# An adaLN transformer block: value rows permuted over partitions, one load of six rows a partition for each tile, value products out of place, and a new instruction order

## The chip, the cores and the metric

The kernel runs on one core of one Trainium2 chip. The core has TensorE (PE in the profile: matmuls; PEld is its weight load), VectorE (DVE), ScalarE (ACT), GpSimd (POOL), and SyncE (SP), which here only issues DMAs. The engines run side by side and meet at semaphores; each runs its own instructions in order. The metric is the time of one execution in microseconds on the device, median of several runs.

## The reference

One block of a diffusion transformer: 2048 tokens, width 512, 32 heads of 16, a sliding dilated attention in which each token sees itself and seven earlier tokens at distances 2, 4, ..., 14, and a gated FFN of width 1792. Inputs are bf16.

```python
mod = (silu(c) @ w_mod)            # six vectors of 512: sa, ca, ga, sb, cb, gb
h = layernorm(x) * (1 + ca) + sa
q, k, v = split(h @ wqkv)          # 32 heads of 16
# for each token and head: 8 logits q.k at distances 0, 2, ..., 14, softmax, sum of the 8 weighted v
x = x + ga * (attention(q, k, v) @ wo)
h = layernorm(x) * (1 + cb) + sb
x = x + gb * ((silu(h @ w1) * (h @ w3)) @ w2)
```

Tokens before the start are masked with -1e9.

## The kernel before

The 2048 tokens are 16 tiles (T) of 128, one token a partition. `_build` describes every operation once, with its engine, what it reads and writes and from which pool of buffers its result comes; a list written out at the end of the file (`ORDER`, and `SLOTS` for the buffers) fixes the order in which each engine issues its operations and the buffer each value takes. `place` and `synchronize` turn the list into instructions with semaphore waits. So the order is fixed by hand, or rather by an offline planner, and nothing is rearranged at run time.

The stages, which the order interleaves:

- Loads by SP: x (tiles 0 and 1 singly, 2 and 3 together, then four by four), `w_mod` in parts (the first 1024 columns in four quarters), `wqkv` in three parts, then `wo`, `w1`, `w3`, `w2`.
- Modulation (L482, L485 on PE): it needs the first four quarters of `w_mod`. [...]
- First layernorm: DVE makes statistics (L540, L541), POOL the reciprocal root (L545, L547), DVE normalises (L552), PE transposes (L612), and ACT or DVE applies scale and shift (L620, L627). The last group of four tiles is transposed by DMA instead.
- Projections: Q and K with the weights stationary, so that they come out with features on partitions and tokens along the row (L664, evicted by ACT at L672 and L673), V with tokens on partitions (L683, evicted at L693). Each V tile is stored to a scratch tensor in DRAM, one DMA of 128 rows a tile.
- Attention, in blocks of two tiles (the last of four). *Logits*: DVE multiplies q by k, eight offsets at once (L714, 4096 elements a partition); PE sums the 16 features of a head with a 0/1 matrix into four groups of 32 partitions (L725, 16 matmuls of 32 rows a tile). *Softmax*: on DVE and ACT in PSUM (L737, L742, L755, L767, L769, L770), then a 32 by 32 transpose on DVE (L774), which leaves the weights in the order of V's rows. *Values*: four DMAs of 256 KB a tile load V from the scratch tensor with each pair of tokens' eight offsets spread over partitions (1 MB a tile, each V row eight times), DVE multiplies in place by the weights (L796), PE sums the eight offsets with a 0/1 matrix (L805), ACT evicts (L811), a DMA transposes, PE multiplies by `wo` (L829), and DVE adds to x and sums the row for the second layernorm (L833).
- Second layernorm: DVE and POOL make bias and scale (L562 nm, L572, L573, L574 nb), ACT squares and normalises (L566, L577), the first two groups of two tiles are transposed by PE, the others by DMA (four DMAs a group) and scaled by ACT (L597).
- FFN in groups of tiles 0 to 1, 2 to 3, 4 to 7, 8 to 11 and 12 to 15: up and gate (L845), activation (L851), product (L855, L856, L859), down (L888, and L876 in half rows for tiles 14 and 15), residual on DVE (L904), and one store a tile, or a half tile for 14 and 15.

V-load buffers: two of 8 KB a partition, and a third one laid over `wqkv` once that is no longer needed (`vsh_x`). Logits products have two buffers, V tiles six, attention weights three, output rows four.

The code around the V load and its product is this:

```python
        for q in range(4):
            p.dma(lambda q=q: vv.at[:, 2 * q:2 * q + 2, :],
                  bass.AP(v_dram, (PAD + T * P + 32 * q) * D, [[2 * D, 16], [-DIL * D, W], [1, 2 * D]]), ...
        def av(e):
            a_w = bass.AP(val.at, i * 8 * H, [[2 * 8 * H, P], [H, 8], [0, DH], [1, H]])
            v_w = bass.AP(vv.at, 0, [[8 * D, P], [D, 8], [H, DH], [1, H]])
            return e.tensor_tensor(v_w, v_w, a_w, ALU.mult)
```

Of the kernel before, what the change touches and what calls it, by code (L numbers as in the profile page):

```python
# [7 lines left out]
ALU = mybir.AluOpType  # L8
# [62 lines left out]
def packet_ns(size):  # L71
    return {256: 18, 512: 27, 768: 36, 1024: 48, 2048: 92}[size]


class Program:
# [41 lines left out]
    def dma(self, out, in_, key, packets, r=(), w=(), part=(), after=(), eng="sp", cost=450, group=None, transpose=False,  # L117
# [13 lines left out]
        ns = 600 if transpose else each * ((PACKET if pre == () and not SHIFTED else 84) if again else packet_ns(size)) + 170 * len(pre)  # L131
# [139 lines left out]
PACKET = 122  # L271
SHIFTED = False
# [3 lines left out]
AVCOL = frozenset(range(16))  # L276
# [5 lines left out]
def _build(p, A_x, A_wqkv, A_wo, B_w1, B_w3, B_w2, c, w_mod, out):  # L282
# [4 lines left out]
    x_view = x2d.rearrange("(t p) d -> p t d", p=P)  # L287
# [14 lines left out]
    vb = [sb([P, D], bf, f"v{i}") for i in range(6)]  # L302
    vshb = [sb([P, 8, D], bf, f"vsh{i}") for i in range(2)]
    pqb = [sb([P, W, KT, P], bf, f"pq{i}") for i in range(2)]
    NSM = 3
    atb = [sb([P, 2, 32, W], bf, f"attn{i}") for i in range(NSM)]
    alb = [sb([P, 2, 8, H], bf, f"al{i}") for i in range(3)]
# [9 lines left out]
    ind = sb([P, 2, 16, 2], bf, "ind")  # L317
    before = sb([P, 2, W, 4, 8], bf, "before")
# [27 lines left out]
    vsh_x = nc.alloc_sbuf_tensor_at("sb_vshx", [P, 8, D], bf, offset=nc.lookup_mloc(wqkv).addr)  # L346

    v_dram = nc.dram_tensor("v_scratch_dram", (PAD + S, D), bf)
    skew = nc.dram_tensor("skew_dram", (NT, 16, 4160), bf) if SHIFTED else None
# [48 lines left out]
    p.op("pool", lambda e: e.memset(ind[:], 0.0), 100, k, w=[vind])  # L398
    for r in range(2):
        p.op("pool", lambda e, r=r: e.memset(ind[:, r, :, r], 1.0), 100, k, w=[vind])  # L400
    for edge, mult in ((0, 1), (W - 1, -1)):
        p.op("pool", lambda e, edge=edge, mult=mult: e.affine_select(
            out=ind[:], in_=ind[:], compare_op=ALU.is_ge, fill=0.0, base=edge, pattern=[[0, 2], [-W * mult, 16], [0, 2]],
            channel_multiplier=mult), 250, k, w=[vind])
    p.op("pool", lambda e: e.memset(before[:], 0.0), 250, k, w=[vbefore])
    for q in range(2):
        p.op("pool", lambda e, q=q: e.affine_select(out=before[:, q], in_=before[:, q], compare_op=ALU.is_ge, fill=BEFORE, base=8 * q,
                                                    pattern=[[-DIL, W], [32, 4], [1, 8]], channel_multiplier=0), 400, k, w=[vbefore])
# [11 lines left out]
    def split_rows(a, row):  # L420
        return bass.AP(a.tensor, a.offset + row * D, [[D, 2], [2 * D, P // 2], [1, D]])

    for T in range(2):
        p.dma(x_sb[:, T, :], x_view[:, T, :], ("load", 1), (128, 1024), w=[vx[T]])
# [3 lines left out]
    p.dma(x_sb[:, 2:4, :], x_view[:, 2:4, :], ("load", 27), (256, 1024), w=vx[2:4])  # L428
# [4 lines left out]
    for g in range(1, 4):  # L433
        p.dma(x_sb[:, 4 * g:4 * g + 4, :], x_view[:, 4 * g:4 * g + 4, :], ("load", 5 + g), (512, 1024), w=vx[4 * g:4 * g + 4])
# [216 lines left out]
    def proj_qk(gi, Ts, kind, vh):  # L651
# [6 lines left out]
        for ft in range(KT):  # L658
            k = ("qk"[kind], 4 * gi + ft)
            vp = Val("ps_qk", psum)  # L660

            def mm(e, ts, ft=ft, vp=vp):
                for t in ts:
                    ins = e.matmul(bank(vp)[:, 0:n], wqkv[:, t, kind * D + ft * P:kind * D + (ft + 1) * P], vh.at[:, t, 0:n],  # L664
                                   start=(t == ORDER[0]), stop=(t == ORDER[-1]))
                return ins

            proj(mm, n, k, vh, vp, vwq[kind])

            def ev(e, ft=ft, vp=vp):  # L670
                if kind == 0:
                    return e.activation(dstv.at[:, ft, at0:at0 + n], bank(vp)[:, 0:n], ACT.Copy, scale=SCALE)  # L672
                return e.activation(kT[:, ft, PAD + 512 * cch + at0:PAD + 512 * cch + at0 + n], bank(vp)[:, 0:n], ACT.Copy)  # L673

            p.op("act", ev, c_act(n), k, r=[vp], part=[dstv])

    def proj_v(T, tt, vh):
        k = ("v", T)
        vp = Val("ps_v", psum)

        def mm(e, ts):
            for t in ts:
                ins = e.matmul(bank(vp), vh.at[:, t, tt * P:(tt + 1) * P], wqkv[:, t, 2 * D:3 * D], start=(t == ORDER[0]),  # L683
                               stop=(t == ORDER[-1]))
            return ins

        proj(mm, D, k, vh, vp, vwq[2])
        vt = Val("v", vpool)

        def ev(e):  # L690
            dst = bass.AP(vt.at, 0, [[D, P], [H, DH], [1, H]])
            src = bass.AP(PALL, bank(vp).offset, [[8 * 512, P], [1, DH], [DH, H]])
            return e.activation(dst, src, ACT.Copy)  # L693

        p.op("act", ev, c_act(512), k, r=[vp], w=[vt])
        vd = Val("vd")
        p.dma(v_dram[PAD + T * P:PAD + (T + 1) * P, :], lambda: vt.at[:], k, (128, 1024), r=[vt], w=[vd], cost=400, store=True)
        vv_dram[T] = vd
# [4 lines left out]
    def logits(Ts):  # L703

        vl = Val("ps_l", psum)
        for i, T in enumerate(Ts):
# [10 lines left out]
            def red(e, i=i, T=T, vp=vp):  # L717
                c0 = vl.at * 512 + i * W * 32
                if T == 0:
                    for q in range(2):  # L720
                        e.matmul(PALL[32 * q:32 * q + 32, c0:c0 + W * 32], ones[:, 0:32], before[:, q].rearrange("p w c t -> p (w c t)"),
                                 start=True, stop=False, tile_position=(0, 32 * q))
                for ft in range(KT):
                    for q in range(4):
                        ins = e.matmul(PALL[32 * q:32 * q + 32, c0:c0 + W * 32], E_sb[:, ft, :], bass.AP(vp.at, ft * P + 8 * q, [[W * KT * P, P], [KT * P, W], [32, 4], [1, 8]]),  # L725
                                       start=(ft == 0 and (T > 0 or q > 1)), stop=(ft == KT - 1), tile_position=(0, 32 * q))
# [35 lines left out]
    def softmax(Ts, vl, ve, vx_):  # L762
# [7 lines left out]
        p.op("dve", lambda e: e.tensor_tensor(ve.at[0][:, 0:n], bass.AP(PALL, bank(vl).offset, [[8 * 512, P], [W * 32, n], [1, 32], [32, W]]),  # L770
                                              bass.AP(ve.at[2], 0, [[64, P], [32, n], [1, 32], [0, W]]), ALU.mult),
             74 + 267 * n, k, r=[vr, vx_], w=[va], hold=[ve, vl], lead=o, lock=False)
        val = Val("al", alpool)
        p.op("dve", lambda e: e.transpose(bass.AP(val.at, 0, [[2 * 8 * H, P], [H, 2], [2 * H, 4 * n], [1, H]]),  # L774
                                          bass.AP(ve.at[0], 0, [[2 * W * 32, P], [8, 2], [16, 16 * n], [1, 8]])),
             60 + 267 * n, k, r=[va], w=[val], hold=[ve], lead=o, lock=False).again = True
        return val

    def values(T, i, val):

        vv = Val("vsh", vshpool)
        loads = []
        for q in range(4):
            pre = []
            if SHIFTED and q == 0:
                for a, b in ((0, 12), (12, 16)):
                    pre.append((bass.AP(skew, (T * 16 + a) * 4160, [[4160, b - a], [1, 4096]]),
                                bass.AP(B_w2.tensor, B_w2.offset + (T % 7 * 16 + a) * 8192, [[8192, b - a], [1, 4096]])))
            p.dma(lambda q=q: vv.at[:, 2 * q:2 * q + 2, :],
# [251 lines left out]
```

## Time and profile before

| | us |
|---|---|
| median of three runs | 244.26 |
| lowest, highest | 243.66, 245.57 |
| profiled execution, own time | 243.52 |
| profiled execution, span | 241.1 |
| granted clock, mean | 0.993 |

The span runs from the first to the last instruction of the profiled execution. "Busy" is the time in which an engine had an instruction under way; matmuls overlap, so the mean duration of one is longer than the distance from one to the next, and a busy PE can still be waiting for a fraction of a microsecond between two of them. A line such as `L796 DVE ... x12 | 27.3, 2286 | 4.2 <-DMA ...` is a group: line of the kernel, engine, output and input, count, busy time in us, mean ns of one, and the idle time of the engine just before these instructions with what ended it. SPq is SP's queue: the time to issue a DMA, not to move its data. Most of the DMA traffic is V loads (16 tiles of 1 MB); the attention spreads from about 24 to 182 us of the span, and PE runs projections and FFN around it.

### The profile page before, as it was taken

The numbers are of one execution on the slowest core, as the hardware profiler recorded it, in microseconds if no ns is written. First come the engines' busy times: TensorE is split into PE (matmuls) and PEld (weight loads), VectorE is DVE, ScalarE is ACT, GpSimd is POOL, SyncE is SP. The second block draws the span as 40 slices with busy tenths as digits, with TensorE's granted clock in tenths as the row PEclk, the third lists the DMA queues.
The fourth block names the chain that finished last, engine by engine and source line by source line (L and its number), as shares of the span: only waits on it lengthen the run. The fifth ranks groups of instructions, "written<-read, shape, count | busy, mean of one in ns | idle before, by whom it ended". The sixth has DMA issues, their size and how long they took to land.

```text
span 241.1 us, 4282 instructions
## 1 busy us (share of the span) xinstructions
PE 233.3 (97%) x1670; PEld 119.8 (50%) x1670; DVE 172.3 (71%) x281; ACT 153.2 (64%) x305; POOL 26.8 (11%) x55
## 2 busy tenths in 40 slices
PE   6699999999999999999899999999999999999995
PEld 1468644444576768564344344443334444444464
DVE  6599999999998999999999896518423414213832
ACT  2369665889998996772897759644576952242100
POOL 3354930001002000121000001100002000000000
PEclk9799999999999999999999999999999999999999
DMA  5999999499599699499996516872040021100011
GB/s 161 356 298 343 270 285 242 105 304 345 178 228 271 196 270 216 92 215 137 253 248 154 162 33 149 140 210 70 0 122 11 22 67 48 42 0 0 0 57 54
DMA packets 44123, 38.30 MB, mean 159 GB/s; under 512 B 19512, under 2 KB 34888, under 8 KB 44104
## 3 DMA queue, kind: packets, MB, share of 16 engines
q1 hardware_dynamic: 44096, 38.04, 61.9%
q8 instruction: 13, 0.21, 0.4%
q14 instruction: 6, 0.05, 0.1%
q10 hardware_dynamic: 8, 0.00, 0.0%
HBM read 29.62 MB, written 4.21 MB: 140 GB/s over the span
## 4 chain that ended last, share of the span: by engine, by line
PE 77%; DMA 8%; DVE 6%; ACT 4%; SPq 2%; POOL 1%; issue 1%; DVEq 0%
PE pall L845 34%; PE pall L888 13%; PE pall L664 11%; PE pall L683 6%; PE pall L829 4%; DMA sb_vsh<-v_scratch_dram 3%; PE pall L876 3%; PE pall L805 2%; PE pall L725 2%; DMA sb_wm_s<-in_w_mod_dram 2%; SPq L127 2%; PE pall L612 2%; DMA sb_h<-sb_xn 1%; ACT sb_xn L577 1%; DMA sb_ot<-sb_oa 1%; ACT sb_h L597 1%
## 5 line engine op out<-in xcount | busy, mean ns | idle before, releaser
L845 PE MATMUL pall<-sb_h,sb_w 128*128 128x512 bf16 (+1 forms) x560 | 102.3, 337 | 0.8 <-ACT sb_h L597 0.7
L845 PEld LDWEIGHTS pall<-sb_h,sb_w 128*128 128x128 bf16 x560 | 51.5, 98 | 49.6 <-ACT sb_sg L851 4.9
L851 ACT ACTIVATE sb_sg<-pall 128x512 bf16<-128x512 f32 (+1 forms) x70 | 34.7, 517 | 26.7 <-PE pall L845 19.7
L888 PE MATMUL pall<-sb_w,sb_hh 128*128 128x512 bf16 x196 | 44.7, 379 | 0.2 <-DVE sb_w L929 0.2
L714 DVE TENSOR_TENSOR sb_pq<-sb_q,sb_kT 128x4096 bf16<-128x4096 bf16 x16 | 36.3, 2282 | 0.2 <-ACT sb_q L672 0.2
L855 ACT ACTIVATE sb_hh<-pall 128x256 bf16<-128x256 f32 (+1 forms) x56 | 26.3, 495 | 7.8 <-PE pall L845 7.8
L664 PE MATMUL pall<-sb_h,sb_wqkv 128*128 128x512 bf16 (+1 forms) x160 | 31.1, 337 | 0.0
L888 PEld LDWEIGHTS pall<-sb_w,sb_hh 128*128 128x128 bf16 x196 | 18.9, 98 | 23.1 <-ACT sb_sg L851 0.9
L796 DVE TENSOR_TENSOR sb_vsh<-sb_vsh,sb_al 128x4096 bf16<-128x4096 bf16 x12 | 27.3, 2286 | 4.2 <-DMA sb_vsh<-v_scratch_dram 4.2
L904 DVE TENSOR_TENSOR sb_o<-pall,sb_x 128x512 bf16<-128x512 f32 (+1 forms) x18 | 11.1, 629 | 19.6 <-PE pall L888 13.2
L856 DVE TENSOR_TENSOR sb_hh<-sb_sg,sb_hh 128x256 bf16<-128x256 bf16 (+1 forms) x56 | 18.0, 349 | 6.4 <-ACT sb_hh L855 4.4
L859 DVE TENSOR_TENSOR sb_hh<-sb_sg,pall 128x512 bf16<-128x512 bf16 x14 | 8.9, 684 | 16.0 <-PE pall L845 16.0
L664 PEld LDWEIGHTS pall<-sb_h,sb_wqkv 128*128 128x128 bf16 x160 | 14.2, 98 | 11.9 <-ACT sb_kT L673 0.6
L620 ACT ACTIVATE sb_h<-pall,sb_modc 128x256 bf16<-128x256 bf16 (+1 forms) x22 | 13.7, 666 | 9.2 <-DVE sb_modc L495 7.2
L572 POOL TENSOR_SCALAR sb_rs<-sb_var 128x2 f32<-128x2 f32 x8 | 3.3, 423 | 145.6 <-ACT sb_xn L566 145.6
L597 ACT ACTIVATE sb_h<-sb_h,sb_modc 128x512 bf16<-128x512 bf16 x16 | 11.8, 804 | 10.1 <-DMA sb_h<-sb_xn 10.1
L833 DVE SCALAR_TENSOR_TENSOR sb_x<-pall,sb_x 128x512 bf16<-128x512 f32 x16 | 10.8, 681 | 8.7 <-PE pall L829 8.5
L829 PE MATMUL pall<-sb_wo,sb_ot 128*128 128x512 bf16 x64 | 16.5, 380 | 0.1
L683 PE MATMUL pall<-sb_wqkv,sb_h 128*128 128x512 bf16 x64 | 16.4, 387 | 0.0
L577 ACT ACTIVATE sb_xn<-sb_x,sb_nb,sb_rs 128x512 bf16<-128x512 bf16 x16 | 12.5, 822 | 3.0 <-DVE sb_nb L574 3.0
L566 ACT ACTIVATE sb_xn<-sb_x,sb_nm 128x512 bf16<-128x512 bf16 x16 | 11.4, 717 | 3.2 <-DVE sb_nm L562 3.2
L673 ACT ACTIVATE sb_kT<-pall 128x512 bf16<-128x512 f32 (+1 forms) x20 | 9.7, 521 | 3.3 <-PE pall L664 3.3
(82 smaller groups left out, 227.5 us busy)
## 6 DMA issues: line engine op xcount, KB each, us to landing
sb_vsh<-v_scratch_dram SPq DMA_DIRECT2D x48, 256.0 KB, 4.8
sb_vshx<-v_scratch_dram SPq DMA_DIRECT2D x16, 256.0 KB, 4.8
sb_w<-in_B_w_dram SPq DMA_DIRECT2D x6, 512.0 KB, 6.9
sb_w<-in_B_w_dram SPq DMA_DIRECT2D x6, 384.0 KB, 6.1
v_scratch_dram<-sb_v SPq DMA_DIRECT2D x16, 128.0 KB, 5.1
out_dram<-sb_o SPq DMA_DIRECT2D x14, 128.0 KB, 1.8
sb_wqkv<-in_A_wqkv_dram SPq DMA_DIRECT2D x3, 512.0 KB, 8.5
sb_x<-in_A_x_dram SPq DMA_DIRECT2D x3, 512.0 KB, 8.0
```

What stands on the lines that cost most here:

```text
L577: p.op("act", lambda e, vn=vn, T=T: e.activation(vn.at[:], x_sb[:, T, :], ACT.Identity, bias=nb[:, T, :], scale=rs[:, NT + T, :]), c_act(5 ...
L597: return e.activation(vh.at[:, ft, 0:n * P], vh.at[:, ft, 0:n * P], ACT.Identity, bias=modc[:, 8 * which + ft:8 * which + ft + 1], scale=m ...
L664: ins = e.matmul(bank(vp)[:, 0:n], wqkv[:, t, kind * D + ft * P:kind * D + (ft + 1) * P], vh.at[:, t, 0:n], start=(t == ORDER[0]), stop=(t ...
L683: ins = e.matmul(bank(vp), vh.at[:, t, tt * P:(tt + 1) * P], wqkv[:, t, 2 * D:3 * D], start=(t == ORDER[0]), stop=(t == ORDER[-1]))
L714: return e.tensor_tensor(vp.at[:], in0, in1, ALU.mult)
L796: return e.tensor_tensor(v_w, v_w, a_w, ALU.mult)
L829: ins = e.matmul(bank(vy), vt.at[:, ft, :], wo[:, ft, :], start=(ft == 0), stop=(ft == KT - 1))
L845: ins = e.matmul(bank(vp)[:, 0:n], wt[:, t, fi * P:(fi + 1) * P], vh.at[:, t, 0:n], start=(t == 0), stop=(t == KT - 1))
L851: p.op("act", lambda e: e.activation(vt.at[:, 0:n], bank(vgp)[:, 0:n], ACT.Silu), c_act(n), k, r=[vgp], w=[vt], table="silu")
L855: p.op("act", lambda e: e.activation(vh_.at[:, 0:n], bank(vup)[:, 0:n], ACT.Copy), c_act(n), k, r=[vup], w=[vh_])
L856: p.op("dve", lambda e: e.tensor_tensor(vh_.at[:, 0:n], vt.at[:, 0:n], vh_.at[:, 0:n], ALU.mult), 60 + n * 69 // 128, k, r=[vt], w=[vh_], ...
L888: ins = e.matmul(bank(vz), vhh[fi].at[:, tt * P:(tt + 1) * P], w2[:, fi, :], start=(fi == 0), stop=(fi == NF - 1))
```

## The change

Within a tile, token and partition are permuted: token 4j + c of a tile sits on partition 32c + j. To that end x is loaded in four DMAs of 32 partitions each (every fourth row), V is stored likewise, two tiles at a time with four DMAs a pair, Q and K are written back in token order by the eviction, and the output store puts the rows back in order with one DMA whose destination has four as its first dimension. Partition (j, pair of offsets) of the V load then needs six consecutive V rows: four tokens, at two offsets two rows apart. So one DMA a tile, with 6 KB a partition, replaces four with 2 KB, 768 KB instead of 1 MB a tile. DVE writes the value product to another buffer, taken from the pool of the logits products, which grows from two to three buffers; V-load buffers are freed by the product instead of by PE's reduction, and shrink to 6 KB. The softmax's last product is split in two, one for each half of the offsets, so that the DVE transpose reads and writes contiguously. The logits reduction reads its products with a step of four elements. The first-tile mask needs one matmul instead of two. V tiles have three buffers of two tiles (instead of six of one), attention weights two (instead of three). Some switches that had one setting are removed. `ORDER` and `SLOTS` are new throughout; among other things one third of `wqkv` is now the first DMA on SP, ahead of x, and value products and logits products are interleaved anew.

```diff
-    for T in range(2):
-        p.dma(x_sb[:, T, :], x_view[:, T, :], ("load", 1), (128, 1024), w=[vx[T]])
+    def load_x(T, n, key, engs):
+        loads = []
+        for c in range(4):
+            p.dma(x_sb[32 * c:32 * c + 32, T:T + n, :],
+                  bass.AP(x2d.tensor, x2d.offset + (T * P + c) * D, [[4 * D, 32], [P * D, n], [1, D]]), key, (32 * n, 1024),
+                  part=vx[T:T + n], eng=engs[c], group=loads)
+    load_x(0, 2, ("load", 1), ("sp", "sp", "sp", "sp"))
...
             def ev(e, ft=ft, vp=vp):
+                src = bass.AP(PALL, bank(vp).offset, [[8 * 512, P], [P, n // P], [32, 4], [1, 32]])
                 if kind == 0:
-                    return e.activation(dstv.at[:, ft, at0:at0 + n], bank(vp)[:, 0:n], ACT.Copy, scale=SCALE)
+                    return e.activation(bass.AP(dstv.at, ft * 512 + at0, [[KT * 512, P], [P, n // P], [1, 4], [4, 32]]), src,
+                                        ACT.Copy, scale=SCALE)
...
-        p.dma(v_dram[PAD + T * P:PAD + (T + 1) * P, :], lambda: vt.at[:], k, (128, 1024), r=[vt], w=[vd], cost=400, store=True)
+        for c in range(4):
+            p.dma(bass.AP(v_dram, (PAD + Ts[0] * P + c) * D, [[4 * D, 32], [P * D, 2], [1, D]]),
+                  lambda c=c: vt.at[32 * c:32 * c + 32, :, :], ("v", Ts[1]), (64, 1024), r=[vt], part=[vd], cost=400, store=True,
+                  group=stores)
...
-                        ins = e.matmul(PALL[32 * q:32 * q + 32, c0:c0 + W * 32], E_sb[:, ft, :], bass.AP(vp.at, ft * P + 8 * q, [[W * KT * P, P], [KT * P, W], [32, 4], [1, 8]]),
+                        ins = e.matmul(PALL[32 * q:32 * q + 32, c0:c0 + W * 32], E_sb[:, ft, :], bass.AP(vp.at, ft * P + 32 * q, [[W * KT * P, P], [KT * P, W], [1, 4], [4, 8]]),
...
+        for wf in range(2):
+            o = p.op("dve", lambda e, wf=wf: e.tensor_tensor(
+                bass.AP(ve.at[0], wf * 128, [[2 * W * 32, P], [W * 32, n], [1, 128]]),
+                bass.AP(PALL, bank(vl).offset + 32 * wf, [[8 * 512, P], [W * 32, n], [1, 32], [64, 4]]),
+                bass.AP(ve.at[2], 0, [[64, P], [32, n], [1, 32], [0, 4]]), ALU.mult),
...
-        for q in range(4):
-            p.dma(lambda q=q: vv.at[:, 2 * q:2 * q + 2, :],
-                  bass.AP(v_dram, (PAD + T * P + 32 * q) * D, [[2 * D, 16], [-DIL * D, W], [1, 2 * D]]), ("vl", T), (128, 2048),
+        p.dma(lambda: vv.at[:], bass.AP(v_dram, (PAD + T * P - 2) * D, [[4 * D, 32], [-4 * D, 4], [1, 6 * D]]), ("vl", T), (128, 6144),
+              r=[vv_dram[T]] + ([] if T % 2 else [vv_dram[T - 1]] if T else [vvpad]), w=[vv], cost=640, again=True)
+        vr = Val("pr", pqpool)
...
-            v_w = bass.AP(vv.at, 0, [[8 * D, P], [D, 8], [H, DH], [1, H]])
-            return e.tensor_tensor(v_w, v_w, a_w, ALU.mult)
+            v_w = bass.AP(vv.at, 2 * D, [[6 * D, P], [-2 * D, 2], [D, 4], [1, D]])
+            return e.tensor_tensor(bass.AP(vr.at, 0, [[8 * D, P], [1, 8 * D]]), v_w, a_w, ALU.mult)
...
-        finals.append(p.dma(out2d[T * P:(T + 1) * P, c0:c0 + n], lambda: vo.at[:, 0:n], ("zo", T), (128, 2 * n), r=[vo], cost=400, store=True))
+        finals.append(p.dma(bass.AP(out2d.tensor, out2d.offset + T * P * D + c0, [[D, 4], [4 * D, 32], [1, n]]), lambda: vo.at[:, 0:n],
+                            ("zo", T), (512, 2 * n), r=[vo], cost=400, store=True))
```

More of the change, by code (lines that the diff above doesn't have):

```diff
@@ L825, in values @@
+        p.dma(lambda: vt.at[:], lambda: va.at[:], ("ac", T), (128, 1024), r=[va], w=[vt], cost=1250, transpose=True)
         vy = Val("ps_y", psum)
@@ L916, in _build @@
         proj_qk(gi, Ts, 1, vh)
-        for i, T in enumerate(Ts):
-            proj_v(T, i, vh)
+        for i in range(0, len(Ts), 2):
+            proj_v(Ts[i:i + 2], (i, i + 1), vh)
     gate(0)
```

144 lines of the change are left out of this document (56 added, 88 removed), and 116 rows, old and new, of tables (ORDER, SLOTS).

## The prediction

> **What bounds the kernel now.** I read the page first (busy times, DMA slices), then the timeline of PE, then the waits of PE and DVE, the groups, and last the chain that ended last around 80 and 110 us.
>
> ```profile
> span 241.1 us, 4282 instructions
> PE 233.3 (97%) x1670; PEld 119.8 (50%) x1670; DVE 172.3 (71%) x281; ACT 153.2 (64%) x305; POOL 26.8 (11%) x55
> DMA  5999999499599699499996516872040021100011
> ```
>
> PE is busy for 233.3 of 241.1 us, so only 7.8 us of the span are PE idle. DMA is nearly full in most slices up to the 22nd (132 us) and light after. The PE timeline shows where the 7.8 us lie (start, length, line, count, idle before it):
>
> ```profile
> 1.81 2.32 PE L503 MATMUL pall<-sb_ones 128*128 128x512 bf16 x5 [1.81 <-DVE sb_ones L383]
> 8.47 0.18 PE L482 MATMUL pall<-sb_mbase,sb_ident 128*128 128x8 bf16 x1 [1.91 <-DMA sb_wm_s<-in_w_mod_dram]
> 10.17 1.27 PE L612 MATMUL pall<-sb_ident,sb_xn 128*128 128x128 bf16 x10
> 11.66 3.20 PE L683 MATMUL pall<-sb_wqkv,sb_h 128*128 128x512 bf16 x12
> ...
> 84.89 1.67 PE L888 MATMUL pall<-sb_w,sb_hh 128*128 128x512 bf16 x7 [0.20 <-DVE sb_w L929]
> ...
> 116.46 0.61 PE L805 MATMUL pall<-sb_vshx,sb_ind 128*32 128x512 bf16 x8 [0.22 <-DVE sb_vshx L796]
> 117.81 7.08 PE L845 MATMUL pall<-sb_h,sb_w 128*128 128x512 bf16 x32 [0.74 <-ACT sb_h L597]
> ...
> 152.69 7.72 PE L888 MATMUL pall<-sb_w,sb_hh 128*128 128x512 bf16 x35
> 160.25 1.03 PE L829 MATMUL pall<-sb_wo,sb_ot 128*128 128x512 bf16 x4
> ...
> 233.77 4.75 PE L876 MATMUL pall<-sb_w,sb_hh 128*128 128x256 bf16 x42
> ```
>
> Idle at the start is 1.81 + 1.91 plus 0.2; in the whole interior 0.20 + 0.22 + 0.74 = 1.2; at the end 241.1 - 238.5 = 2.6. A 512-column matmul in steady state takes (160.25 - 152.69)/35 = 0.216 us. Going through this timeline's rows from 16.71 us to the end (140 rows; first and last: 16.71 and 233.77) and comparing start-to-start times with count x 0.216 (half for 256 columns, a quarter for the 32-column reductions), 7.7 us are over: 3.8 at the 25 blocks of 32-column reductions, where PE changes its tiling (1.0 of it the two idles at 116 and 117), and 3.9 spread thinly. So the matmul work, which the change leaves alone, fixes about 230 us; a better order can win little more than the 1.2 us of idle and part of the 3.9.
>
> **The change, part by part.**
>
> *Start.* PE's first needed work is the modulation, released by the DMA of its weights.
>
> ```profile
> 0.79 1.39 SPq L127 DMA_DIRECT2D sb_x<-in_A_x_dram  x3
> 2.22 1.85 SPq L127 DMA_DIRECT2D sb_wm_s<-in_w_mod_dram  x4
> 6.00:12.00 6.00, 4.09 (x55) 2.89 (x54) 3.56 (x11) 1.83 (x5) 2.10 (x6) 0.76 1.03 356
> 12.12 0.69 DVE L540 BATCH_NORM_STATS2 sb_st<-sb_x 128x6 f32<-128x512 bf16 x1 [0.34 <-DMA sb_x<-in_A_x_dram]
> 24.50 2.29 DVE L714 TENSOR_TENSOR sb_pq<-sb_q,sb_kT 128x4096 bf16<-128x4096 bf16 x1 [0.22 <-ACT sb_q L672]
> ```
>
> (The third row is a window: busy time of PE, PEld, DVE, ACT, POOL, then clock 0.76, DMA share 1.03, 356 GB/s.) SP spends 1.85/4 = 0.46 us on an issue. Now the last quarter of the modulation weights is SP's 7th DMA, with 1.5 MB up to it; in the new order it is the 13th, with 2.0 MB (512 KB of wqkv went to the front, and each x load became four pieces). Issues end at 0.79 + 13 x 0.46 = 6.8 us, which is earlier than the bytes: 0.5 MB more at 356 GB/s is 1.5 us, so the last quarter comes at 8.5 + 1.5 = 10.0, its 8 matmuls and modc take some 0.4, and the first projection can start at about 10.8. Before, it started at 11.66, because PE did transposes for tiles 2 and 3 first (10.17); these eight (0.1 us each at that clock) now come later. Good end: -0.4. Bad end: if pieces of 32 partitions load at half the rate of whole tiles, 0.5 MB of x costs 1.5 us more: +1.1. No row shows the rate of a piece alone, so I take +0.2, nearer the good end, because the large wqkv transfer in front covers the small issues.
>
> *Middle.* x of tiles 4 to 7 has 3.0 MB up to its end instead of 2.5, so DVE's row at 12.12 moves by 1.5 us, of which the normalising of tiles 2 and 3 (moved into the gap) fills 0.8: DVE's first logits product (24.50) comes 0.7 to 1.5 us later. From there DVE is the engine that PE's order leans on:
>
> ```profile
> L714 DVE TENSOR_TENSOR sb_pq<-sb_q,sb_kT 128x4096 bf16<-128x4096 bf16 x16 | 36.3, 2282 | 0.2 <-ACT sb_q L672 0.2
> L796 DVE TENSOR_TENSOR sb_vsh<-sb_vsh,sb_al 128x4096 bf16<-128x4096 bf16 x12 | 27.3, 2286 | 4.2 <-DMA sb_vsh<-v_scratch_dram 4.2
> L770 DVE TENSOR_TENSOR sb_attn<-pall,sb_ssum 128x512 bf16<-128x512 f32 x8 | 5.5, 684 | 0.1
> L904 DVE TENSOR_TENSOR sb_o<-pall,sb_x 128x256 bf16<-128x256 f32 x4 | 1.7, 425 | 5.0 <-PE pall L876 5.0
> 82.78 7.77 DMA sb_vsh<-v_scratch_dram
> ...
> 109.23 0.17 DVE sb_nb L574
> ...
> 111.50 3.29 DMA sb_h<-sb_xn
> ...
> 114.82 2.94 ACT sb_h L597 x4
> ```
>
> The last four rows are from the chain: the normalising of tiles 6 and 7 (109.23), its transposes and ACT's scaling are what PE waits for at 117.81. Up to that nb instruction DVE runs 12 logits products, 9 value products and 5 softmaxes in both orders. The value product out of place costs what the logits product does (also out of place, also with a backward step: 2282 against 2286): nothing. The softmax's last product in two halves is 2 x 425 - 684 = +166 ns, 5 times by then, 0.8 us. What can go is DVE's wait for V, 4.2 us in all, 0.3 of it after that point: one 768 KB load replaces four of 256 KB, and the chain's V load took 7.77 us. Sum for the nb instruction: +0.7 to +1.5, +0.8, and between 0 and -3.9: from -2.4 to +2.3. The FFN of 117.81 moves with it, but not to before 116.5, where PE's own work ends: -1.3 to +2.3. I take 0, the middle.
>
> *SP's queue.* 64 V-load issues become 16, 16 V stores become 32, six x loads become 20.
>
> ```profile
> L127 SPq DMA_DIRECT2D sb_vsh<-v_scratch_dram x48: 515/594/1319, 20.3 to 159.7; - x48
> L127 SPq DMA_DIRECT2D v_scratch_dram<-sb_v x16: 344/588/1528, 16.0 to 124.5; - x16
> L693 ACT ACTIVATE sb_v<-pall 128x512 bf16<-128x512 f32 x16 | 9.4, 607 | 1.9 <-PE pall L683 1.9
> L672 ACT ACTIVATE sb_q<-pall 128x512 bf16<-128x512 f32 x12 | 6.8, 601 | 2.0 <-PE pall L664 2.0
> ```
>
> -48 x 0.594 + 16 x 0.588 + 14 x 0.46 = -12.7 us of SP time, spread; it acts only through the waits for V and the transposes, so it is in the range above. The first store of a pair now waits for the second tile's eviction (one more projection, 4 x 0.216, and 0.6 on ACT: 1.5 us); behind it stand V loads and transposes on SP, and DVE waits for those. SP's 12.7 us hide it; without them, up to 1.5 us at one place. Value products now take one of three buffers shared with the logits products; a product that finds none waits for PE's reduction, with DVE's whole queue behind it: at most one block of PE work (7 x 0.216 = 1.5 us), in the same range. Q and K are evicted with a rearranged write: V's eviction, rearranged on its read side, took 607 against 601 ns, so nothing; the fewer constants of POOL are hidden before 8.47.
>
> *End.* The output rows of a tile now go to four interleaved runs, the first dimension of the destination being four.
>
> ```profile
> out_dram<-sb_o SPq DMA_DIRECT2D x14, 128.0 KB, 1.8
> out_dram<-sb_o SPq DMA_DIRECT2D x4, 64.0 KB, 1.5
> sb_wo<-in_A_wo_dram SPq DMA_DIRECT2D x4, 128.0 KB, 7.2
> v_scratch_dram<-sb_v SPq DMA_DIRECT2D x16, 128.0 KB, 5.1
> ```
>
> 64 KB more cost 1.8 - 1.5 = 0.3 us. At best the last store stays at 1.5 us (0); if only a quarter of the DMA engines carries it, its moving part is 4 x 0.3 and the end comes 0.9 us later. No row shows such a store: +0.5, the middle. [...]
>
> *Sum:* +0.2 + 0 + 0.5 = +0.7. On the profiled execution (span 241.1, its own time 243.52) that is 244.2; that execution lies 0.74 under the median of the three times (244.26), so the median forecast is 245.0.
>
> **Rivals.**
>
> *The waits go and the order closes up (faster).* With the V waits gone, PE loses its 1.2 us of idle and some 2.4 of the 3.9 thin losses, and the start takes its good end: -3.6 - 0.4 + 0.5 = -3.5, 240.8. For it: DVE waits 4.2 us for V. Against it: PE was idle only 1.2 us while that happened.
>
> *x in 32-partition pieces loads at half the rate (slower).* All 2 MB of x at 178 instead of 356 GB/s take 5.9 us more. The start takes +1.1; tiles 4 to 15 reach DVE later, and after the cover that DVE's other work gives I put the first logits at 3.5 us later rather than 0.7 to 1.5; with 0.8 for softmax and half of the V waits gone (-2.0) the FFN at 117.81 moves by 2.3, and the last store by 0.9: +3.2, 247.5. It decides from about 250 GB/s downwards. For it: 32-partition loads of wo took 7.2 us for 128 KB, against 5.1 for the V stores; against it: both ran under a full DMA. [...]
>
> *The strided read slows the reductions (slower).* PE's logits reduction now reads its products with a step of four elements instead of runs of eight.
>
> ```profile
> 27.61 0.44 PE pall L725 x16
> ```
>
> Sixteen of them take 0.44 us, so the 256 take 7.0 us on PE; at half the rate that is +7.0, +7.7 with the forecast: 252. No row shows PE reading with such a step; it decides as soon as a reduction takes over 0.6 us.
>
> **How the numbers follow.** Forecast 0.50, closing up 0.20, half-rate x 0.22, strided read 0.08. The forecast's own range is the middle's -1.3 to +2.3 around 245.0: 243.7 to 247.3. Eight in ten: 240.8 leaves out the lower half of the first rival (0.10), 248.0 the strided read; 240.8 to 248.0. 1% (2.4 us) is about what a measurement can tell from no change: under 241.8 falls nearly all of the first rival, 0.19; over 246.7 fall most of the half-rate case, the strided read and a little of the forecast, 0.31; 0.50 remains.
>
> **What would show it.** Start: PE's first projection near 11.3 to 11.9, and the wait of DVE for x under 2.5 us. Middle: DVE's wait for V under 2 us, and the first 512-column FFN matmul within 2.3 us of 117.8. End: landing of a 64 KB store, 1.5 or over 2.2 us. Reductions: 16 in 0.44 us, or 0.9. The prediction is wrong if PE shows an idle of over 3 us in its interior, or if the thin losses fall below 2 us.

## The result, and the profile after

The changed kernel takes 265.38 us (median of four runs, 264.28 to 265.95) against 243.96 for the kernel before on the same chip: ratio 1.0865, 95% interval 1.0796 to 1.0935. The forecast was 245.0, its range 240.8 to 248.0. The change costs 21 us, more than any rival gave. Every ratio here divides the mean time by that of the kernel before run beside it (median 243.9 to 244.9 us from one session to the next) and leaves out the few executions in a slower state, which the ranges of times include.

The page of the changed kernel (the span, the engines' busy times, the chain that ended last):

```profile
span 263.5 us, 4267 instructions
PE 244.4 (93%) x1669; PEld 121.2 (46%) x1669; DVE 172.9 (66%) x289; ACT 169.8 (64%) x303; POOL 26.6 (10%) x52
q1 hardware_dynamic: 37448, 33.84, 45.2%
PE 69%; ACT 21%; DMA 5%; issue 1%; DVE 1%; SPq 1%; POOL 0%; POOLq 0%; DVEq 0%
```

The last two of these lines in the page of the kernel before (the queue that carries nearly all DMAs, and the chain):

```profile
q1 hardware_dynamic: 44096, 38.04, 61.9%
PE 77%; DMA 8%; DVE 6%; ACT 4%; SPq 2%; POOL 1%; issue 1%; DVEq 0%
```

PE now lacks 19.1 us of the span (7.8 before). ScalarE's busy time rose from 153.2 to 169.8 us, and it holds 21% of the chain (4% before). The DMA load fell as intended, by 4.2 of 38.0 MB, and that bought nothing that shows. (The V loads were 16.8 of these 38.0 MB, the largest part but less than half.) The groups of the lines that the change touched (kept apart by shape), and under them those of the kernel before that the prediction does not show:

```profile
L668 ACT ACTIVATE sb_q<-pall 128x512 bf16<-128x512 f32 x12 | 16.1, 1362 | 2.1 <-PE pall L659 2.1
L670 ACT ACTIVATE sb_kT<-pall 128x512 bf16<-128x512 f32 x12 | 15.4, 1374 | 1.4 <-PE pall L659 1.4
L670 ACT ACTIVATE sb_kT<-pall 128x256 bf16<-128x256 f32 x8 | 5.3, 796 | 2.0 <-PE pall L659 2.0
L668 ACT ACTIVATE sb_q<-pall 128x256 bf16<-128x256 f32 x8 | 5.2, 853 | 0.0
L726 PE MATMUL pall<-sb_pq,sb_E 128*32 128x256 bf16 x256 | 15.6, 393 | 0.0
L792 DVE TENSOR_TENSOR sb_pq<-sb_vsh,sb_al 128x4096 bf16<-128x4096 bf16 x13 | 29.5, 2285 | 1.5 <-PE pall L801 1.5
L772 DVE TENSOR_TENSOR sb_attn<-pall,sb_ssum 128x256 bf16<-128x256 f32 x16 | 6.5, 418 | 0.0
```

```profile
L672 ACT ACTIVATE sb_q<-pall 128x256 bf16<-128x256 f32 x8 | 3.1, 442 | 0.4 <-PE pall L664 0.4
...
L673 ACT ACTIVATE sb_kT<-pall 128x512 bf16<-128x512 f32 x12 | 7.0, 600 | 2.9 <-PE pall L664 2.9
L673 ACT ACTIVATE sb_kT<-pall 128x256 bf16<-128x256 f32 x8 | 2.7, 402 | 0.3 <-PE pall L664 0.3
...
L725 PE MATMUL pall<-sb_pq,sb_E 128*32 128x256 bf16 x256 | 8.9, 274 | 0.0
```

Two groups have become dear. A 512-column eviction of Q or K takes 1362 to 1374 ns instead of 600; the four eviction rows together hold ScalarE for 42.0 us, before 19.6 (with the 6.8 of Q's 512 columns). And a matmul of the logits reduction takes 393 ns on the mean instead of 274. The value product and the halves of the softmax product cost what the prediction said, and DVE's wait for V is gone.

PE's timeline (start, length, line, count, idle before it) shows where this lands:

```profile
11.94 2.32 PE L659 MATMUL pall<-sb_h,sb_wqkv 128*128 128x256 bf16 x10
...
28.01 1.04 PE L683 MATMUL pall<-sb_wqkv,sb_h 128*128 128x512 bf16 x4 [0.56 <-ACT sb_q L668]
...
61.51 1.04 PE L813 MATMUL pall<-sb_wo,sb_ot 128*128 128x512 bf16 x4 [0.59 <-ACT sb_kT L670]
...
64.48 1.92 PE L726 MATMUL pall<-sb_pq,sb_E 128*32 128x256 bf16 x32
...
77.14 1.04 PE L683 MATMUL pall<-sb_wqkv,sb_h 128*128 128x512 bf16 x4 [0.64 <-ACT sb_q L668]
...
137.65 7.08 PE L829 MATMUL pall<-sb_h,sb_w 128*128 128x512 bf16 x32
```

The first projection comes at 11.94 (before 11.66), the first 512-column FFN matmul at 137.65 (before 117.81). So 19.6 of the 22.4 us of span are lost between these two. Q, K and V are projected there until about 85 us, and PE's short waits name ScalarE's evictions: the idles that the whole timeline lists between 12 and 89 us add up to 9.2 us, 9.0 of them ended by an eviction of Q, K or V, where the kernel before had 1.2 us of idle in its whole interior. The same stretch in windows of 6 us (busy time of PE, PEld, DVE, ACT, POOL, each with its count; clock, DMA share, GB/s), first of the changed kernel, then of the kernel before:

```profile
24.00:30.00 6.00, 4.60 (x34) 2.62 (x32) 2.09 (x7) 6.00 (x11) 0.15 (x1) 1.00 0.93 324
54.00:60.00 6.00, 5.40 (x53) 2.42 (x51) 4.62 (x3) 6.00 (x9) 0.00 (x0) 1.00 0.62 109
```

```profile
54.00:60.00 6.00, 6.00 (x34) 2.94 (x33) 5.91 (x8) 6.00 (x13) 0.92 (x2) 1.00 1.05 344
```

The last row is one that the prediction should have shown: between 54 and 60 us ScalarE was already busy for all 6.00 us before the change (and for 5.98 and 5.94 us in the next two windows). Its 64% over the span is an average; in this stage it had no slack, so a surcharge on its evictions there can go straight into the time.

### The profile page after: what moved, and what is told of

It is laid out like the page before. It is cut to its first block, busy times and chain, and to the rows that moved or that the text cites. A ratio compares the mean times of both kernels' runs of the same rounds, so it can differ in the third digit from the quotient of the medians.

```text
span 263.5 us, 4267 instructions
## 1 busy us (share of the span) xinstructions
PE 244.4 (93%) x1669; PEld 121.2 (46%) x1669; DVE 172.9 (66%) x289; ACT 169.8 (64%) x303; POOL 26.6 (10%) x52
## 4 chain that ended last, share of the span: by engine, by line
PE 69%; ACT 21%; DMA 5%; issue 1%; DVE 1%; SPq 1%; POOL 0%; POOLq 0%; DVEq 0%
PE pall L829 35%; PE pall L872 11%; ACT sb_q L668 7%; ACT sb_kT L670 6%; PE pall L726 5%; PE pall L659 5%; PE pall L813 4%; PE pall L683 4%; PE pall L801 2%; DMA sb_ot<-sb_oa 2%; DMA sb_h<-sb_xn 2%; ACT sb_h L592 2%; ACT sb_h L615 2%; ACT sb_v L692 1%; DMA sb_x<-in_A_x_dram 1%; PE pall L860 1%
## 5 line engine op out<-in xcount | busy, mean ns | idle before, releaser
L872 PE MATMUL pall<-sb_w,sb_hh 128*128 128x512 bf16 x196 | 43.8, 379 | 0.0
L659 PE MATMUL pall<-sb_h,sb_wqkv 128*128 128x512 bf16 (+1 forms) x160 | 33.8, 348 | 2.3 <-ACT sb_q L668 1.2
L839 ACT ACTIVATE sb_hh<-pall 128x256 bf16<-128x256 f32 (+1 forms) x56 | 27.0, 501 | 11.8 <-PE pall L829 11.6
L792 DVE TENSOR_TENSOR sb_pq<-sb_vsh,sb_al 128x4096 bf16<-128x4096 bf16 x13 | 29.5, 2285 | 1.5 <-PE pall L801 1.5
L670 ACT ACTIVATE sb_kT<-pall 128x512 bf16<-128x512 f32 (+1 forms) x20 | 20.7, 1142 | 3.5 <-PE pall L659 3.5
L668 ACT ACTIVATE sb_q<-pall 128x512 bf16<-128x512 f32 (+1 forms) x20 | 21.0, 1159 | 2.1 <-PE pall L659 2.1
L615 ACT ACTIVATE sb_h<-pall,sb_modc 128x256 bf16<-128x256 bf16 (+1 forms) x22 | 12.6, 648 | 9.0 <-DVE sb_modc L490 8.5
L726 PE MATMUL pall<-sb_pq,sb_E 128*32 128x256 bf16 x256 | 15.6, 393 | 0.0
```

The source lines that it names most:

```text
L668: return e.activation(bass.AP(dstv.at, ft * 512 + at0, [[KT * 512, P], [P, n // P], [1, 4], [4, 32]]), src, ACT.Copy, scale=SCALE)
L670: return e.activation(bass.AP(kT, ft * (PAD + S) + PAD + 512 * cch + at0, [[KT * (PAD + S), P], [P, n // P], [1, 4], [4, 32]]), src, ACT.Copy)
L792: return e.tensor_tensor(bass.AP(vr.at, 0, [[8 * D, P], [1, 8 * D]]), v_w, a_w, ALU.mult)
L839: p.op("act", lambda e: e.activation(vh_.at[:, 0:n], bank(vup)[:, 0:n], ACT.Copy), c_act(n), k, r=[vup], w=[vh_])
L872: ins = e.matmul(bank(vz), vhh[fi].at[:, tt * P:(tt + 1) * P], w2[:, fi, :], start=(fi == 0), stop=(fi == NF - 1))
```

## Experiments

**Theory:** ScalarE pays for writing with a step of four elements, PE for reading with one; these two cost most of the 21 us, and x in pieces and the output store the rest. **Rivals:** a permuted eviction is slow on whichever side the step is; or the new order of the instructions is what is slow.

### The eviction's step moved to the read side

```diff
-src = bass.AP(PALL, ..., [[8 * 512, P], [P, n // P], [32, 4], [1, 32]])
+src = bass.AP(PALL, ..., [[8 * 512, P], [P, n // P], [1, 32], [32, 4]])
-bass.AP(dstv.at, ft * 512 + at0, [[KT * 512, P], [P, n // P], [1, 4], [4, 32]])
+dstv.at[:, ft, at0:at0 + n].rearrange("p (i j c) -> p i j c", j=32, c=4)   # written in a row; kT likewise
```

> The changed kernel with one edit: the evictions of Q and K write in a row and pick the token order on the read side, from PSUM, with a step of 32 elements. Theory A (ScalarE pays for writes with a step of four elements): an eviction of 512 columns goes from 1362 to 1374 ns back to about 600, ScalarE saves 22 us, the first 512-column FFN matmul comes at about 124 instead of 137.65 (the reductions keep their part), and the time is 247 to 253 us. Rival B (any permuted eviction is slow, whichever side has the step): evictions stay over 1.2 us and the time near 265. Rival C (the new order is at fault, ScalarE is only late with it): evictions fall to 600 ns but the time stays over 258.

Measured: 251.17 us (250.44 to 253.3), ratio to the kernel before 1.0296 (1.0215 to 1.0376). The groups of this kernel:

```profile
L668 ACT ACTIVATE sb_q<-pall 128x512 bf16<-128x512 f32 x12 | 7.3, 613 | 1.4 <-PE pall L659 1.4
L670 ACT ACTIVATE sb_kT<-pall 128x512 bf16<-128x512 f32 x12 | 6.8, 607 | 1.6 <-PE pall L659 1.6
```

The same elements go to the same places with as many loops; the two inner loops are exchanged, so that the step, now of 32 elements, is on the PSUM side: 607 to 613 ns. So neither the permutation nor the number of its dimensions is what costs, but the step of the write into SBUF (1362 to 1374 ns in the changed kernel). 14.2 us come back (13.9 by the ratios), with the FFN matmul at 123.14; both rivals fall as explanations of the larger part.

### The reduction in runs

```diff
-... bass.AP(vp.at, ft * P + 32 * q, [[W * KT * P, P], [KT * P, W], [1, 4], [4, 8]])
+... bass.AP(vp.at, ft * P + 32 * q, [[W * KT * P, P], [KT * P, W], [1, 32]])
 # softmax's last product, now for each tile and half, picks the order in PSUM:
+bass.AP(PALL, ... + 32 * wf, [[8 * 512, P], [1, 4], [4, 8], [64, 4]])
```

> The changed kernel with one edit: the logits reductions read their products in runs of 32 tokens instead of with a step of four elements, and the softmax's last product picks the order when it reads PSUM (an instruction for each tile and half, so 32 instead of 16). Theory: 16 reductions take 0.44 us again instead of 0.86 to 0.97. If PE sets the time everywhere, that is 16 x 0.45 = 7 us less, 258. If ScalarE's evictions set it up to 88 us, only the seven or so tiles reduced after them gain, about 3 us, and the time is 261 to 263. No gain at all would mean that the reductions are not slowed by the step.

Measured: 261.40 us (261.06 to 262.12), ratio 1.0704 (1.0637 to 1.0770): 4.0 less than the changed kernel, the expected partial gain. That the rest of PE's saving went into longer waits for ScalarE is what the expectation argued; it was not measured by itself.

### Both

> Both edits together. If the two steps of four elements are the whole of what was lost, the time is that of the kernel before within 1.5%, 241 to 247 us, with the first 512-column FFN matmul within 3 us of 117.8. If the new order or the loads of x in four pieces cost something of their own, it stays over 249.

Measured: 247.54 us (247.28 to 247.79), ratio 1.0129 (1.0055 to 1.0204). Span 245.8, and on PE's timeline:

```profile
66.26 1.06 PE L726 MATMUL pall<-sb_pq,sb_E 128*32 128x256 bf16 x32
...
120.98 6.85 PE L833 MATMUL pall<-sb_h,sb_w 128*128 128x512 bf16 x31 [0.85 <-ACT sb_h L592]
...
235.70 6.28 PE L864 MATMUL pall<-sb_w,sb_hh 128*128 128x256 bf16 x56
```

A pair of tiles is reduced in 1.06 us again (1.92 in the changed kernel), and the FFN matmul comes 16.7 us earlier. The two steps are worth 17.8 of the 21.4 us. What is left is 1.3%; the time lies 0.5 us above the expected 241 to 247, and the FFN matmul is 3.2 us late, at the edge of the 3 that were allowed (31 of 32 matmuls are recorded in its row, so it may have begun 0.2 us earlier). Something smaller of its own remains.

### Each step alone, in the kernel before

The same write in the kernel before (its old order, loads and V path):

> The kernel before with one part of the change alone: Q and K are evicted with the rearranged write, four runs of 32 with a step of four elements. Tokens of Q and K then stand in another order than the rest expects, so the logits are of other pairs of tokens; the work is the same in kind and amount. Theory A: evictions take about 1365 ns instead of 600 and the time rises by 10 to 16 us, to 254 to 260. Theory C (the new order makes the slow evictions matter): evictions slow down as much but the time rises by less than 5 us.

Measured: 257.51 us (256.92 to 259.3), ratio 1.0553 (1.0476 to 1.0630), evictions of 1350 to 1358 ns, the FFN matmul at 132.10. So the slow write costs 12.6 us in the old order and 14.2 in the new one (13.5 and 13.9 by the ratios): the new order is not what makes it matter.

The strided read alone, in the kernel before:

> The kernel before with one part of the change alone: the logits reductions read their products with a step of four elements. Tokens then stand in another order than the mask and the softmax's transpose expect; the work is the same. Theory: 16 reductions take 0.87 us instead of 0.44, and because PE sets the time almost everywhere here, all of 16 x 0.43 = 6.9 us shows: 249.5 to 251.5. Rival (as between the two edits of the changed kernel, where undoing it gave 3.6): 247 to 248.5.

Measured: 248.74 us (248.51 to 249.01), ratio 1.0208 (1.0178 to 1.0239). Its PE timeline:

```profile
50.93 1.92 PE L725 MATMUL pall<-sb_pq,sb_E 128*32 128x256 bf16 x32
...
121.20 7.08 PE L845 MATMUL pall<-sb_h,sb_w 128*128 128x512 bf16 x32
```

The reductions take what was expected, but 4.6 us show rather than 6.9, between the two expectations. The span grew by 5.2 us, 1.7 less than the reductions. The row at 121.20 has no idle before it, where the kernel before waited 0.74 (and 0.22 shortly ahead of it), but over the whole span PE's idle fell by only 0.4 us, from 7.8 to 7.4 (246.3 less 238.9 busy). The other 1.3 us are thin savings between matmuls, and their cause stays open.

### The price of the step

A step of two elements at both places of the kernel before:

> The kernel before with two doses of a smaller step: Q and K are evicted in two runs of 64 with a step of two elements, and the logits reductions read their products with a step of two elements instead of runs of eight. Tokens then stand in another order than the mask and the later steps expect; the work is the same. If the price goes with the number of 8-byte or larger pieces that a line of memory is cut into, step two costs about half of step four's surcharge: evictions of 512 columns near 980 ns (600 + 760/2), 16 reductions near 0.66 us. If only steps of over two elements are charged, they stay at 600 ns and 0.44 us. If any step is charged in full, 1360 ns and 0.87 us.

A step of eight:

> The kernel before with a larger step at both places: Q and K are evicted in eight runs of 16 with a step of eight elements, and the logits reductions read with a step of eight elements. Tokens stand in another order than the later steps expect; the work is the same. Step two gave 751 to 763 ns and no surcharge on PE, step four 1350 to 1374 and 0.87 us. If the price keeps growing with the step (so with the number of bytes spanned), the evictions take over 2 us and 16 reductions over 1.2 us; if every element is charged by itself from a step of four on, they stay at step four's figures.

One run each: 245.70 us with step two, 304.22 with step eight. First the groups and one reduction of step two, then of step eight:

```profile
L675 ACT ACTIVATE sb_kT<-pall 128x512 bf16<-128x512 f32 x12 | 8.8, 763 | 2.6 <-PE pall L664 2.6
L673 ACT ACTIVATE sb_q<-pall 128x512 bf16<-128x512 f32 x12 | 8.5, 751 | 1.3 <-PE pall L664 1.1
```

```profile
49.84 1.06 PE L728 MATMUL pall<-sb_pq,sb_E 128*32 128x256 bf16 x32
```

```profile
L673 ACT ACTIVATE sb_q<-pall 128x512 bf16<-128x512 f32 x12 | 29.9, 2627 | 0.4 <-PE pall L664 0.4
L675 ACT ACTIVATE sb_kT<-pall 128x512 bf16<-128x512 f32 x12 | 29.7, 2601 | 2.0 <-PE pall L664 1.9
```

```profile
80.15 3.62 PE L728 MATMUL pall<-sb_pq,sb_E 128*32 128x256 bf16 x32
```

| step in elements | eviction of 512 columns, ns | reduction of two tiles, us |
|---|---|---|
| 1 | 600 | 1.06 |
| 2 | 751 to 763 | 1.06 |
| 4 | 1350 to 1374 | 1.92 |
| 8 | 2601 to 2627 | 3.62 |

From step two to eight the duration nearly doubles with each doubling of the step, on ScalarE and on PE; the first doubling, from one to two, adds a quarter on ScalarE and nothing on PE. Of the expectations, "keeps growing with the step" held at eight. At two, "about half of step four's surcharge" did not hold: it is 20% on ScalarE and nothing on PE, so on PE alone "only steps of over two elements are charged" held. The pieces from which that half was worked out were a supposition; no run shows them.

### x in pieces

What is left with both edits sits in the front (3.2 us at the FFN matmul) and in the tail. x loaded whole:

```diff
-for c in range(4):
-    p.dma(x_sb[32 * c:32 * c + 32, T:T + n, :], bass.AP(x2d.tensor, ..., [[4 * D, 32], [P * D, n], [1, D]]), ...)
+p.dma(x_sb[:, T:T + n, :], bass.AP(x2d.tensor, ..., [[D, P], [P * D, n], [1, D]]), ...)
```

> The kernel with both edits (247.54), and x loaded in whole tiles again, one DMA where the change has four, in the order of the rows. The permutation of x is left out, so tokens are matched with the wrong neighbours; the work is the same. In the trace of the kernel with both edits the chain of waits starts with 27 issues on SP up to 14.2 us and an x load that lands at 21.4, and the first 512-column FFN matmul comes at 120.98. Theory: 14 issues fewer take 6 us off SP's head; DVE's first logits product comes at 24.5 instead of 25.5, the FFN matmul at 118 to 119.5, and the time is 244.5 to 246. Rival (what is left comes from the new order of the instructions): 247 to 248 and the FFN matmul at 120.5 or later.

Pieces issued from two queues (`("sp", "act", "sp", "act")`):

> The kernel with both edits, x in the same 32-partition pieces as there, but every second piece is issued by ScalarE's queue instead of SP's. If SP's time for the issues is what x in pieces costs, this gains about as much as whole loads of x, to 245 to 246.5. If it is the rate of a 32-partition piece (half of a whole tile's), nothing is gained: 247 to 248.

Pieces of neighbouring rows (row `32 * c + j` instead of `4 * j + c`):

> The kernel with both edits, x in the same four pieces of 32 partitions from SP, but each piece takes 32 neighbouring rows of a tile instead of every fourth one. The permutation of x is left out, as in the run with whole loads (245.71, FFN matmul at 119.07). Theory (pieces of 32 partitions load more slowly, whatever rows they take): as with both edits, 247 to 248, the FFN matmul at about 121, and some 305 GB/s between 6 and 12 us. Rival (the step over the rows in DRAM is what is slow): as with whole loads, 245.5 to 246, 119, and 356 GB/s.

| x | us | ratio | FFN matmul at |
|---|---|---|---|
| pieces, every fourth row | 247.54 | 1.0129 (1.0055 to 1.0204) | 120.98 |
| whole tiles | 245.71 | 1.0066 (1.0028 to 1.0103) | 119.07 |
| pieces, half of them from ScalarE's queue | 248.08 | 1.0153 (1.0064 to 1.0241) | 121.10 |
| pieces of neighbouring rows | 247.70 | 1.0144 (1.0092 to 1.0195) | 121.34 |

Whole tiles gave the expected time and FFN matmul. The window from 6 to 12 us (last two numbers: DMA share, GB/s) of pieces of every fourth row, of whole tiles, of pieces from two queues, and of neighbouring rows:

```profile
6.00:12.00 6.00, 2.87 (x45) 1.60 (x46) 4.82 (x15) 0.54 (x2) 3.40 (x10) 0.88 1.00 305
```

```profile
6.00:12.00 6.00, 4.36 (x50) 2.63 (x50) 4.89 (x17) 1.02 (x2) 3.49 (x10) 1.00 1.06 356
```

```profile
6.00:12.00 6.00, 2.31 (x35) 1.44 (x34) 3.19 (x9) 0.00 (x0) 2.54 (x8) 0.82 1.06 263
```

```profile
6.00:12.00 6.00, 3.20 (x45) 1.89 (x44) 4.62 (x15) 0.34 (x1) 2.95 (x10) 1.00 1.02 295
```

The DMA engines are busy all the time in all four (shares of 1.00 to 1.06), but move 263 to 305 GB/s in pieces and 356 in whole tiles. (From 12 to 18 us the gap is smaller: 243 to 268 against 290.) Freeing SP of half the issues gained nothing (that expectation failed), though the rate fell to 263 GB/s in that run, which could hide a small gain. Neighbouring rows gained nothing. So it is the load in pieces, not its rows, and nothing speaks for SP's time; whether the 32 partitions of a piece or the fourfold number of DMAs is what lowers the rate was not separated. It costs about 1.8 us here (1.5 by the ratios), and the FFN matmul comes 1.9 to 2.3 us earlier with whole tiles; the intervals of the ratios with pieces overlap that with whole tiles, so the size is less certain than the rates. Half the rate, 178 GB/s, is not what these windows show, in which other loads run beside the pieces; the rate of a piece alone no run shows.

### The output store

The chain of the changed kernel at its end ("issue" is time in which an engine waits for nothing that the profile shows):

```profile
256.33 0.77 DVE sb_o L888 x2
257.10 0.02 issue
257.11 2.44 DMA out_dram<-sb_o
259.56 0.03 issue
...
260.00 0.43 DVE sb_o L888
```

The last row on DVE waits for the buffer of a store issued 2.4 us before (the new slots give it that one), so that it starts 2.14 us after the row before it, 0.6 longer than the usual 1.53; from its end (260.43) to the end of the span it is 3.1 us, 2.1 before (238.98 to 241.1). The half-tile stores of the last two tiles as pieces:

```diff
-bass.AP(out2d.tensor, ..., [[D, 4], [4 * D, 32], [1, n]]) <- vo.at[:, 0:n]
+for c in range(4):   # c = 0, 1 from SP, 2, 3 from ScalarE
+    bass.AP(out2d.tensor, ... + c * D, [[4 * D, 32], [1, n]]) <- vo.at[32 * c:32 * c + 32, 0:n]
```

> The kernel with both edits, and the half-tile stores of the last two tiles as four DMAs of 32 partitions each (two from SP, two from ScalarE) instead of one whose destination has four as its first dimension. If the first dimension of four keeps a store on a quarter of the DMA engines, the stretch from the last matmul's end to the end of the span falls from 3.8 to about 3 us and the last store lands in about 1.5 instead of 2.4; time 246.5 to 247. If the stores' layout does not matter, the tail stays or grows by an issue (0.45), 247.5 to 248.

Measured: 246.65 us (245.74 to 248.83), ratio 1.0129 (1.0085 to 1.0173): no difference that can be told from the run with both edits. A piece lands in 1.8 to 1.9 us, but a second issue goes ahead of the last, and the tail only falls to 2.8 us. So this run settles little. The plain store, with x whole:

> The kernel with both edits, x in whole tiles and the output rows stored in the order of the partitions by one plain DMA. The permutation of x and of the output is left out. Theory (a destination whose first dimension is four takes 0.9 us more for 64 KB): the 64 KB stores land in 1.5 us, the last row waits for no buffer, and from the last row's end on DVE to the end of the span it is 2.1 us instead of 3.1; the time falls by 1.0 to 1.3 from the run with whole loads (245.71), to 244.4 to 244.7, within 0.5% of the kernel before. Rival (the new order itself costs the rest): 245.4 to 246.

Measured: 244.29 us (242.8 to 248.54), ratio 1.0016 (0.9988 to 1.0043), on the DMA rows and DVE's timeline:

```profile
out_dram<-sb_o SPq DMA_DIRECT2D x4, 64.0 KB, 1.5
```

```profile
240.06 0.42 DVE L891 TENSOR_TENSOR sb_o<-pall,sb_x 128x256 bf16<-128x256 f32 x1 [1.10 <-PE pall L863]
```

The last row waits for PE alone and ends at 240.48; the span ends at 242.7, 2.2 us later. The time falls by 1.4 from the run with whole loads (1.2 by the ratios, whose intervals overlap), as the theory had it; with the same slots, no row waits for a buffer any more. How many engines carry the store with four runs no row counts; the 0.9 us for a quarter of them was an estimate in the prediction, and the tail's 3.1 against 2.1 us agrees with it in size.

## Why the prediction was wrong

In the order in which they were undone, the losses by medians are 14.2 us for the write, 3.6 for the read, 1.8 for x, and 1.4 for the store and its buffer; by the ratios, which take out the differences between sessions, 13.9, 4.1, 1.5 and 1.2. Each is the difference of one run to the next, so that they add up from 265.38 to the last run's 244.29 proves nothing by itself. What counts is that this run equals the kernel before (244.16 beside it; ratio 0.9988 to 1.0043), and that write and read alone cost 12.6 and 4.6 us in the old order. What remains to the new order and to the shorter V path is nothing together; whether a small gain of the one pays for a small loss of the other was not separated. One such loss shows in the traces: V tiles now free their three buffers in pairs, and in the kernels with both edits ScalarE waits 3.0 to 5.2 us for a V store to do so, where the kernel before never waits for one. The row of the last run:

```profile
L691 ACT ACTIVATE sb_v<-pall 128x512 bf16<-128x512 f32 x16 | 9.5, 602 | 5.7 <-DMA v_scratch_dram<-sb_v 3.0 <-PE pall L682 2.6
```

- **The step that failed:** "Q and K are evicted with a rearranged write: V's eviction, rearranged on its read side, took 607 against 601 ns, so nothing". The row was of a read from PSUM, and it was used for a write into SBUF. That read row does carry over to a read: 607 to 613 ns. For the write no row of the kernel before existed, so the term needed two ends. It measured +762 to +774 ns on 24 evictions and about +400 on 16; ScalarE's busy time on them rose by 22.4 us (42.0 less 19.6 for the four rows before), of which 14.2 showed in the time. (Its total rose by only 16.6, in part because its other work got shorter: with the step on the read side its groups add up to 168.4 us, 2.7 under the 171.1 of the kernel before.) No rival had ScalarE as the bound, although the window at 54 us showed it full. The prediction's own sign of being wrong, over 3 us of idle in PE's interior, came: 9.2 us up to 89 us, all ended by ScalarE.
- **Strided read:** the mechanism of that rival and its dose were right (twice 0.44 us for 16; the chain of the changed kernel has 32 in 1.74, the row below). Its price of 7.0 was too high: 3.6 to 4.6 showed. In the old order a smaller idle of PE explains 0.4 us of the difference, and the rest stays open. That it came true, at a chance of 0.08, also breaks the premise that the change leaves PE's matmul work alone: the reductions hold PE for 15.6 us instead of 8.9.

```profile
37.49 1.74 PE pall L726 x32
```

- **Start:** +0.2 forecast, 11.94 against 11.66 measured. The number is right, its reason is not: the pieces were to be covered by the wqkv transfer, but with x whole the first projection comes at 10.97 and 11.36, so the pieces cost it something, and a gain of the new order happens to offset that. (The working also gives 10.0 + 0.4 = 10.4, or its 10.8, both earlier than its good end of 11.3.) DVE's wait for x is 4.8 us, not under 2.5 (row below; 1.8 before). The rival that pieces load at half the rate had the direction and nearly the price, not the dose, half the rate, which no run shows: between 6 and 12 us the kernels with pieces move 263 to 305 GB/s, not 178 (the lowest window from 12 to 18 us has 243; that rival was to decide from about 250 downwards), and they lose 1.8 us where the rival had 2.3 (its 3.2 less 0.9 for the store).

```profile
L535 DVE BATCH_NORM_STATS2 sb_st<-sb_x 128x6 f32<-128x512 bf16 x16 | 10.3, 674 | 4.8 <-DMA sb_x<-in_A_x_dram 4.8
```

- **Middle:** the value product (2285 ns), the softmax halves (2 x 418 ns) and the end of the wait for V came as forecast. With both edits, x whole and a plain store, the FFN matmul stands at 119.29, 1.5 later than before and inside the range of -1.3 to +2.3. (The 0 that was taken is the middle of the range before its cut at -1.3; of the cut one it is +0.5.) DVE's first logits product, forecast 0.7 to 1.5 us later than 24.50, started at 25.50, 26.74 and 27.16 in the three runs with both edits and x in pieces from SP: forecast a little too early; in the changed kernel it waited for Q until 29.70.
- **SP's queue:** that its issues are hidden at no cost was not contradicted for x: halving SP's issues of x gained nothing. The fewer issues of V loads were not tried alone.
- **End:** +0.5 forecast between 0 and 0.9; the tail grew by 1.0, just above the upper end. The 0.9 was worked out from a quarter of the DMA engines, which no run shows; what the runs show is that the 64 KB store at the chain's end takes 2.44 to 2.53 us with four runs and lands in 1.5 in the order of the partitions. The late landing also holds a buffer that the new slots give to the last row, which adds 0.6 in the changed kernel and 0.3 with both edits; the prediction did not look at that.
- **Closing up:** the rival that the vanished waits shorten the kernel did not happen. In the run with all four parts undone the V load is one DMA of 768 KB and DVE waits for it nowhere, and the time is that of the kernel before.

A version that beats both kernels did not come out of this: those that keep the permutation throughout are at best 1.3% slower than before (both edits, with or without the split stores).

## What to carry to other kernels

Look at which side of which engine carries the step of a permutation. Here a step of 32 elements on ScalarE's read from PSUM cost about 2% (607 to 613 ns against 600), while a step of four on its write into SBUF more than doubled the instruction (1350 to 1374 ns). A new access pattern without a row in the trace needs a price with two ends, and the cover for it is read from the stage where it runs, not from the engine's share of the whole span. And a wait of an engine that does not set the time (DVE for V, 4.2 us) bought nothing here when it went.

## What the runs showed of the hardware

- ScalarE's writes into SBUF in bf16 take 600, 757, 1362 and 2614 ns for 512 elements with steps of 1, 2, 4 and 8 (means of the rows above, steps 2 and 8 from one run each); 32 of TensorE's matmuls that read with such steps take 1.06, 1.06, 1.92 and 3.62 us. A step of eight elements cost 4.4 times on ScalarE and 3.4 times on TensorE.
- ScalarE's read from PSUM with a step of 32 fp32 elements cost 6 to 13 ns of 600.
- With x in 32-partition pieces the core's DMA moved 295 to 305 GB/s between 6 and 12 us when one queue issued them and 263 when two did, against 356 and 360 with whole tiles, each at a share of 0.99 to 1.08 of the engines' time.
